# Router gates carried through the one-hot products, a state decay on ScalarE, and a new order at the border

## The chip, the cores and the metric

The kernel runs on one core of a Trainium2 chip. The metric is the device time of one execution in microseconds. Engines are named as in the profile: PE (matrix engine), DVE (VectorE), ACT (ScalarE), POOL (GpSimd) and SP (SyncE, which here only issues DMAs).

## The reference

Linear attention with a decaying state (batch 4, 8 heads, 768 tokens, head dimension 48), then a mixture of experts over its 3072 output rows of 384, with one expert per token and a skip gate:

```python
for t in range(S):
    kt, vt, rt, wt = (k[:, :, t], v[:, :, t], r[:, :, t], w[:, :, t])
    cur = np.einsum('bhd,bhe->bhde', u[None] * kt, vt)
    y[:, :, t] = np.einsum('bhd,bhde->bhe', rt, state + cur)
    state = wt[:, :, :, None] * state + np.einsum('bhd,bhe->bhde', kt, vt)
...
do_compute = x @ w_skip > 0
xc = x[do_compute]
logits = xc @ w_gate
e_idx = np.argmax(logits, axis=1)
probs = softmax(logits)
gate_w = probs[np.arange(len(xc)), e_idx]
for e in range(E):
    mask = e_idx == e
    h = np.maximum(xc[mask] @ w1[e], 0.0)
    y[mask] = gate_w[mask, None] * (h @ w2[e])
out[do_compute] = xc + y
```

Eight experts of 384 x 1024 x 384; w_gate's softmax value of the chosen expert is the token's gate.

## The kernel before

**Attention.** There are 24 steps of 128 tokens (4 sequences of 6 chunks). In each, DVE makes decay products by two scans (L396, L414), POOL and DVE scale r and k with them, PE makes the score quarters (psA, L432), DVE masks them (asb, L448) and adds the bonus (psY, L460), and PE multiplies them with v (L496) and adds the state's part (L502). ACT copies psY to xT (L508). The state lives in PSUM as psu; `update` (L470) adds the chunk's kt v, `carry` (L479) multiplies psu by the next chunk's decay q, and `carry_out` (L488) copies it to SBUF as sblk for the next step's L502. `rows_out` (L517) turns xT into output rows and router logits, which SP stores and later gathers read.

**Router.** Steps are routed in three groups, GROUPS = (0, 12), (12, 6), (18, 6). For each, DVE finds the expert of each token and its rank (sg, rall), one-hot rows of the rank are made (`one_hot`, by DVE, or by ACT as the pair off and hot, L633 and L634), and `places` (L651) multiplies the one-hots, as weights, with sg. The result pt (in PSUM, shown as psu) holds, per expert and rank, the token's index in two parts and a flag that the slot is taken. From it come idr and ids, the index lists of the gathers. The token's gate is 1 / sum of the exponentials; `gate_rows` turns it on PE, copies it on ACT and stores it with SP (L610 to L613) to gd in DRAM, and POOL later gathers it for each of 16 tiles of tokens (`gate`, L548, tiles gt).

**Border.** The last group's router runs after the last step. PE fills it with expert 0's first 128 tokens (L159, then L733), which were found early.

**Experts.** Each has up to 256 tokens in two tiles (xg, gathered by POOL), transposed on PE (L953), split into high and low halves xTh and xTl, and multiplied by the first weights (L977 to L979, or L991 where at most 160 tokens came) and the second (L1001, with L1008 for the few tokens of such an expert: e = 2, 6 and 7). The weights come in by SP (L116), are rounded by ACT (w1h, w2h, L135) and completed by DVE or POOL (w1l, w2l, L139). DVE scales by the gate and adds the row (fin, L1088), POOL scatters it (L962). Order on all engines is the program's order; an engine waits in line.

A tile for a later gather is cleared by DVE when the gather is issued, and loads for expert 2 are tied to an earlier copy:

```python
xg[s] = pool.tile([P, DM], F32, tag=f"xg{s % 2}", name=f"xg{s}", bufs=3)
if s < 10:
    nc.vector.memset(xg[s], 0.0)
...
for load in load_weights(2, q):
    beside(load, copied[1])
```

`flags` (L942, L943) sums two checks by two tiny products into psf; it stands ahead of the last expert's last layer-2 products.

Of the kernel before, what the change touches and what calls it, by code (L numbers as in the profile page):

```python
# [20 lines left out]
P = 128  # L21
# [28 lines left out]
          24: ((1, 2), (1, 3))}  # L50
KEYS_AT = {-2: (), -1: (0,), 0: (1,), 1: (2, 3)}
# [21 lines left out]
NV = 3  # L73
# [6 lines left out]
def rwkv_moe_kernel(ctx, tc, wrk, wrk0, vN, uP, wgs, wgp, w12, cst, out):  # L80
# [3 lines left out]
    gd = dram.tile([NT, 1], F32, name="gd")  # L84
# [65 lines left out]
    gts = [keep.tile([P, 1], F32, name=f"gt{s}") for s in range(2 * E)]  # L150
# [17 lines left out]
    with tc.tile_pool(name="att", bufs=2) as att, \  # L168
# [99 lines left out]
        ids = keep.tile([P, 2, E], U32, name="ids")  # L268
        floor = pss[:, :NP * HW // 2].bitcast(BF16)
# [3 lines left out]
        for nm, wd in (("desc", E), ("mx", MG), ("km", MG), ("sm", MG), ("os1", E), ("rank", MG)):  # L273
            o = 396 + sum(z.shape[1] for z in small.values())
            small[nm] = pss[:, o:o + wd]
        tok_ps = pss[:, 512 - 2 * n:].rearrange("p (c q o) -> p c q o", q=2, o=1)
        gall = pers.tile([P, n], F32, name="gall")
# [197 lines left out]
        def carry(i):  # L475
            b, c = seq[i]
            if c == NC - 1:
                return
            nc.vector.tensor_tensor(psu[:, :, :D], psu[:, :, :D],  # L479
                                    work[i + 1]["q"][:, :, 0:1].to_broadcast([P, NP, D]),  # L480
                                    op=ALU.mult)
# [51 lines left out]

        def gather(s, pool):
            if pool:
                xg[s] = pool.tile([P, DM], F32, tag=f"xg{s % 2}", name=f"xg{s}", bufs=3)
                if s < 10:
                    nc.vector.memset(xg[s], 0.0)  # L538
# [7 lines left out]

        def gate(s, rows, index):
            nc.gpsimd.indirect_dma_start(  # L548
                out=gts[s], out_offset=None, in_=gd[:rows],
                in_offset=bass.IndirectOffsetOnAxis(ap=index, axis=0),  # L550
                bounds_check=rows - 1, oob_is_err=False)

        def router(i0, m):
# [74 lines left out]
            def one_hot(c):  # L628
# [6 lines left out]
                if c in by_act:  # L635
# [11 lines left out]
            def places():  # L647
                placed.append(i0)
                for j in (1, 0):
                    for k, c in enumerate(order):  # L650
                        nc.tensor.matmul(pt[:, j], hots[c][:, j * P:(j + 1) * P],  # L651
                                         sg[:, c], start=False, stop=(k == m - 1),
                                         skip_group_check=True)
            if last:
                held.append(places)
# [6 lines left out]
            sm = by("sm", m, 1)  # L662
            vec.tensor_reduce(sm, ex, axis=AX, op=ALU.add)
            yield 1
            vec.reciprocal(gall[:, i0:i0 + m].rearrange("p (c o) -> p c o", o=1), sm)
            yield 1
            if not last:
                grow()
                rare.extend((places, gate_rows))
            else:  # L670
                held.append(gate_rows)
# [211 lines left out]
        for s in (2, 3):  # L883
            gather(s, None)
# [393 lines left out]
```

## Time and profile before

| | |
|---|---|
| median of 3 runs | 277.79 us (277.7 to 278.22) |
| profiled execution | 277.29 us, its span 275.5 us |
| PE busy | 257.7 us (94%) |
| DVE busy | 226.7 us (82%) |
| POOL busy | 213.6 us (78%) |
| ACT busy | 152.3 us (55%) |

The span is the time from the first to the last instruction that the profiler shows; the 1.79 us around it belong to the execution. Shares are of the span. A PE at 94% leaves about 18 us, of which those at the start and after the last product are outside this change. Times in the rows below are microseconds from the span's start.

### The profile page before, as it was taken

How to read it: one execution, taken by the hardware profiler on the slowest of the kernel's cores; microseconds unless marked ns; L12 is line 12 of the kernel's file. 1: busy time of each engine (PE TensorE's matmuls, PEld its weight loads, DVE VectorE, ACT ScalarE, POOL GpSimd, SP SyncE). 2: the span in 40 equal slices, each digit the busy share in tenths (PEclk: the TensorE clock that was granted, in tenths of full speed). 3: DMA queues.
4: the chain of work that ended last, by engine and by line, in shares of the span. 5: the costliest groups of instructions: out<-in, count | busy, mean ns of one | idle time of the engine just before them, and what ended most of it. 6: DMA issues, size and time to landing. Idle time of an engine off the chain costs nothing.

```text
span 275.5 us, 9346 instructions
## 1 busy us (share of the span) xinstructions
PE 257.7 (94%) x3705; PEld 226.8 (82%) x3706; DVE 226.7 (82%) x428; ACT 152.3 (55%) x376; POOL 213.6 (78%) x199
## 2 busy tenths in 40 slices
PE   7899999999989999998999899999999999999990
PEld 2467878888878878786788899996999999999870
DVE  6998699888899999986284529899999979979960
ACT  6133443433445687453543737385893957959810
POOL 7989989999889798689656822696898989876811
PEclk9999999999999999999999999999999999999997
DMA  6979999999999998587945984439698696984001
GB/s 165 248 204 295 269 279 247 280 254 241 284 255 238 286 266 237 145 271 235 338 158 151 348 334 154 140 80 376 257 335 306 192 353 254 329 293 156 37 6 49
DMA packets 24803, 64.38 MB, mean 234 GB/s; under 512 B 4483, under 2 KB 15779, under 8 KB 23206
## 3 DMA queue, kind: packets, MB, share of 16 engines
q1 hardware_dynamic: 21910, 58.40, 69.6%
q0 software_dynamic: 2560, 4.76, 5.2%
q8 instruction: 39, 0.64, 0.9%
q10 hardware_dynamic: 272, 0.39, 0.5%
q14 instruction: 22, 0.18, 0.2%
HBM read 57.21 MB, written 7.88 MB: 236 GB/s over the span
## 4 chain that ended last, share of the span: by engine, by line
PE 63%; DMA 16%; DVE 10%; issue 6%; ACT 2%; POOL 1%; SPq 1%; POOLq 0%; DVEq 0%; ACTq 0%
PE psO L1001 17%; PE psH L991 7%; PE psY L496 5%; PE psA L432 4%; PE psH L977 4%; PE psH L979 4%; PE psH L978 4%; PE psX L517 4%; DMA wrk<-wrk 4%; PE psY L502 3%; DMA r<-w 3%; DVE asb L448 3%; PE psY L456 3%; DMA xg<-out,ids 2%; PE psT L441 2%
## 5 line engine op out<-in xcount | busy, mean ns | idle before, releaser
L391 POOL TENSOR_TENSOR wrk<-wrk 128x512 f32<-128x512 f32 x24 | 36.2, 1509 | 1.7
L139 DVE TENSOR_TENSOR w1l<-r,w1h 128x512 fp32r<-128x512 f32 x31 | 36.6, 1197 | 0.1
L448 DVE TENSOR_TENSOR asb<-psA,c_sb 128x512 f32<-128x512 f32 x48 | 30.8, 682 | 5.0 <-PE psA L432 4.7
L412 POOL TENSOR_TENSOR kq<-wrk,q 128x512 f32<-128x512 f32 x24 | 26.9, 1120 | 10.0 <-DVE q L396 8.1
L1001 PE MATMUL psO<-w2h,hh 128*128 128x384 f32 x96 | 32.8, 342 | 0.0
L962 POOL DMA_INDIRECT out<-fin,ids x16 | 19.6, 1223 | 17.1 <-DVE fin L1088 6.9
L139 POOL TENSOR_TENSOR w2l<-r,w2h 128x512 fp32r<-128x512 f32 x24 | 31.0, 1313 | 2.3 <-ACT w2h L135 2.0
L508 ACT COPY xT<-psY 128x512 f32<-128x512 f32 x24 | 14.0, 585 | 33.7 <-PE psY L502 25.8
L1001 PE MATMUL psO<-w2l,hh 128*128 128x384 f32 x96 | 32.2, 336 | 0.0
L496 PE MATMUL psY<-asb,vN 128*64 128x128 f32 (+1 forms) x384 | 26.1, 276 | 3.0 <-DVE psY L460 2.9
L384 POOL TENSOR_TENSOR rk<-wrk 128x512 f32<-128x512 f32 x22 | 28.1, 1275 | 0.0
L539 POOL DMA_INDIRECT xg<-out,ids x14 | 17.5, 1253 | 13.3 <-DVE xg L538 9.1
L432 PE MATMUL psA<-rp,kq 64*64 64x128 f32 (+1 forms) x768 | 26.3, 252 | 1.3 <-POOL kq L412 1.3
L135 ACT CAST w2h<-r 128x512 fp32r<-128x512 f32 x48 | 27.3, 655 | 0.0
L977 PE MATMUL psH<-xTh,w1h 128*128 128x224 f32 (+1 forms) x96 | 26.9, 280 | 0.0
L979 PE MATMUL psH<-xTh,w1l 128*128 128x224 f32 (+1 forms) x96 | 26.5, 277 | 0.0
L978 PE MATMUL psH<-xTl,w1h 128*128 128x224 f32 (+1 forms) x96 | 26.5, 276 | 0.0
L135 ACT CAST w1h<-r 128x512 fp32r<-128x512 f32 x42 | 25.6, 632 | 1.6 <-DMA r<-w 1.6
L496 PEld LDWEIGHTS psY<-asb,vN 128*64 128x64 f32 (+1 forms) x384 | 20.4, 130 | 5.3 <-DVE psY L460 4.3
L432 PEld LDWEIGHTS psA<-rp,kq 64*64 64x64 f32 x768 | 21.8, 133 | 3.3 <-POOL kq L412 1.7
L1040 DVE SCALAR_TENSOR_TENSOR hl<-psH,hh 128x512 fp32r<-128x512 f32 (+1 forms) x32 | 20.2, 648 | 4.2 <-ACT hh L1039 3.9
L1039 ACT ACTIVATE hh<-psH 128x512 fp32r<-128x512 f32 (+1 forms) x32 | 18.3, 570 | 9.2 <-PE psH L979 6.5
(179 smaller groups left out, 707.0 us busy)
## 6 DMA issues: line engine op xcount, KB each, us to landing
r<-w SPq DMA_DIRECT2D x12, 1536.0 KB, 7.3
wrk<-wrk SPq DMA_DIRECT2D x23, 577.9 KB, 6.6
r<-w SPq DMA_DIRECT2D x12, 512.0 KB, 7.5
wp<-wrk SPq DMA_DIRECT2D x9, 516.0 KB, 8.6
vN<-vN SPq DMA_DIRECT2D x12, 384.0 KB, 4.7
out<-x SPq DMA_DIRECT2D x24, 192.0 KB, 5.4
vt<-wrk SPq DMA_DIRECT2D x24, 96.0 KB, 6.3
vt<-wrk SPq DMA_DIRECT2D x48, 48.0 KB, 4.6
```

Source lines behind the costliest of these rows:

```text
L135: nc.scalar.copy(hi, raw)
L139: eng.tensor_tensor(lo, raw, hi.bitcast(F32), op=ALU.subtract)
L384: (nc.gpsimd if i > 1 else nc.vector).tensor_tensor(rk.rearrange("p a j -> p (a j)"), t[:, R_OFF:K_OFF], t[:, K_OFF:V_OFF], op=ALU.mult)
L391: nc.gpsimd.tensor_tensor(rk1, rk1, two(1, 1, CW), op=ALU.mult)
L412: nc.gpsimd.tensor_tensor(pairs(kq), pairs(wk["k"]), twice(wk["q"][:, :, 1:HW]), op=ALU.mult)
L432: nc.tensor.matmul(psa[g][j:j + HP, a, j:], wk["kq"][rows, a, j:j + HP], wk["rp"][rows, a, j:], start=True, stop=True)
L448: nc.vector.tensor_tensor(s, psa[g], tri.rearrange("p (o j) -> p o j", o=1).to_broadcast([P, NP, P]), op=ALU.mult)
L496: nc.tensor.matmul(quarter(0, a, g, w), head(i, 2 * a + g, w), wk["asb"][g][:, a], start=False, stop=(c == 0), skip_group_check=True)
L977: nc.tensor.matmul(ps, w1h[:, o:o + P], xh, start=(kc == 0), stop=False)
L978: nc.tensor.matmul(ps, w1h[:, o:o + P], xl, start=False, stop=False)
L979: nc.tensor.matmul(ps, w1l[:, o:o + P], xh, start=False, stop=(kc == KC - 1))
L1001: nc.tensor.matmul(pso, h[j, fc][k], w[:, fc * DM:(fc + 1) * DM], start=(i == 0), stop=(i == len(todo) - 1))
```

## The change

Five edits. (1) In steps 12 to 19 that carry a state (12 to 16, 18, 19) the decay of psu is four ACT activations with a scale per partition in place of one DVE product. (2) The gate is cut into three bf16 values, whose sum is the gate in float precision, and these ride as three more columns times eight experts through the places' products; `gates`, one sum out of PSUM, replaces the rows in DRAM and the 16 gathers. In the last group the first 24 columns go first and the gates' 24 in a second set of products. (3) At the border the first one-hot is made by ACT, ids and the gathers of tiles 2 and 3 follow idr at once. (4) Tiles 6 to 9 are cleared in expert 0, and the loads of expert 2's weights wait for the landing of the third gather. (5) The flags' products stand behind the eighth of the last 24 products.

```diff
+BY_ACT = range(12, 20)
...
-NV = 3
+NV = 6
...
@@ carry
+            q = work[i + 1]["q"]
+            if i in BY_ACT:
+                for a in range(NP):
+                    nc.scalar.activation(psu[:, a, :D], psu[:, a, :D], AF.Copy, scale=q[:, a, 0:1])
+                return
             nc.vector.tensor_tensor(psu[:, :, :D], psu[:, :, :D],
...
+        def token_tile(s, pool):
+            xg[s] = pool.tile([P, DM], F32, tag=f"xg{s % 2}", name=f"xg{s}", bufs=3)
+            if s < 10:
+                nc.vector.memset(xg[s], 0.0)
...
-        def gate(s, rows, index):
-            nc.gpsimd.indirect_dma_start(
-                out=gts[s], out_offset=None, in_=gd[:rows],
...
-            def gate_rows():
-                pg = ps1.tile([P, 512], F32, tag="psT", name=f"pg{i0}", bufs=2)[:m, :P]
-                nc.tensor.transpose(pg, gall[:, i0:i0 + m], ident)
-                row = att.tile([MG, P], F32, tag="gate", name=f"gate{i0}", bufs=1)[:m]
-                nc.scalar.copy(row, pg)
-                nc.sync.dma_start(gd[i0 * P:(i0 + m) * P].rearrange("(c p) o -> c (p o)", p=P), row)
+            def weigh():
+                sm, w = by("sm", m, 1), parts_ps[:, :m]
+                vec.tensor_reduce(sm, ex, axis=AX, op=ALU.add)
+                yield 1
+                vec.reciprocal(w[:, :, 0], sm)
+                yield 1
+                for q in range(2):
+                    part = att.tile([P, MG, 1], BF16, tag=f"part{q}", name=f"part{q}_{i0}")[:, :m]
+                    vec.tensor_copy(part, w[:, :, q])
+                    vec.tensor_tensor(w[:, :, q + 1], w[:, :, q], part, op=ALU.subtract)
+                    yield 1
+                vec.tensor_tensor(
+                    sg[:, :, 3:], oh.rearrange("p c (o e) -> p c o e", o=1)
+                    .to_broadcast([P, m, 3, E]), w.to_broadcast([P, m, 3, E]), op=ALU.mult)
...
-            by_act = () if last else [c for c in range(m) if c % 3 if m == MG or c % 2]
+            by_act = (0,) if last else [c for c in range(m) if c % 3 if m == MG or c % 2]
...
-            def places():
+            def places(a=0, b=NV):
...
             if last:
-                held.append(places)
+                held.append(lambda: places(0, 3))
                 while held:
                     yield 1
...
                 gather(1, None)
+                taken = pt[:, :, 2]
+                vec.tensor_scalar(idf, taken, 0.0, BIG, op0=ALU.is_equal, op1=ALU.mult)
+                vec.tensor_tensor(ids, idf, idr, op=ALU.add)
+                for s in (2, 3):
+                    landed.append(gather(s, None))
+            yield from weigh()
+            if last:
+                held.append(lambda: places(3, NV))
+                while held:
+                    yield 0
+                vec.tensor_reduce(gates, pt[:, :, 3:].rearrange("p j q e -> p j e q"), axis=AX,
+                                  op=ALU.add)
+                return
...
             for i, (k, fc, w) in enumerate(todo):
+                if beside and i == FC:
+                    beside()
...
             if e == 0:
+                for s in range(6, 10):
+                    token_tile(s, moe)
                 scatter(0, fin0)
...
-                nc.vector.scalar_tensor_tensor(o, pso, gts[s], xg[s],
+                nc.vector.scalar_tensor_tensor(o, pso, gates[:, j, e:e + 1], xg[s],
...
-                if s == 2 * E - 1:
-                    flags()
...
-                    beside(load, copied[1])
+                    beside(load, landed[-1])
```

Where instructions stand at the border, on DVE. Before, behind the first index list of the last group (pss is a PSUM scratch, gall the gates, few and size_i the expert sizes):

```order
L285 TENSOR_REDUCE pss<-ex_sb 128x6
L285 RECIPROCAL gall<-pss 128x6
L711 TENSOR_TENSOR h0l<-hf_2693,h0h 128x512
L881 TENSOR_SCALAR idf<-psu 128x16
L882 TENSOR_TENSOR ids<-idf,idr 128x16
L886 TENSOR_SCALAR few<-psu 1x8
L887 SCALAR_TENSOR_TENSOR few<-psu,few 1x8
```

And now, at the same place:

```order
L287 TENSOR_SCALAR idf<-psu 128x16
L287 TENSOR_TENSOR ids<-idf,idr 128x16
L287 TENSOR_REDUCE pss<-ex_sb 128x6
L287 RECIPROCAL pss<-pss 128x6
L287 CAST part_18_2781<-pss 128x6
L287 TENSOR_TENSOR pss<-pss,part_18_2781 128x6
L287 CAST part_18_2785<-pss 128x6
L287 TENSOR_TENSOR pss<-pss,part_18_2785 128x6
L287 TENSOR_TENSOR sg_2710<-sg_2710,pss 128x6x24
L287 TENSOR_REDUCE gates<-psu 128x16
L731 TENSOR_TENSOR h0l<-hf_2701,h0h 128x512
L900 TENSOR_SCALAR few<-psu 1x8
```

The index list of tiles 2 and 3 has moved ahead, and the gates' chain stands ahead of h0l and of the sizes.

On PE, between the last group's places and the first gather's transposes, before (w2h and w2l are expert 0's second weights):

```order
L733 MATMUL psO_2759<-w2h_0_1537,h0h 128x384
L733 MATMUL psO_2759<-w2l_0_1538,h0h 128x384
L733 MATMUL psO_2759<-w2h_0_1537,h0h 128x384
L610 MATMUL pg_2764<-c_sb,gall 6x128
L733 MATMUL psO_2759<-w2l_0_1538,h0h 128x384
L733 MATMUL psO_2759<-w2h_0_1537,h0h 128x384
```

And now:

```order
L753 MATMUL psO_2778<-w2h_0_1524,h0h 128x384
L753 MATMUL psO_2778<-w2l_0_1525,h0h 128x384
L753 MATMUL psO_2778<-w2h_0_1524,h0h 128x384
L753 MATMUL psO_2778<-w2l_0_1525,h0h 128x384
L753 MATMUL psO_2778<-w2h_0_1524,h0h 128x384
L665 LDWEIGHTS hot_0_2728
L665 MATMUL psu<-sg_2710,hot_0_2728 128x24
L665 LDWEIGHTS hot_1_2732
L665 MATMUL psu<-sg_2710,hot_1_2732 128x24
```

The gate transpose after the third product is gone, and after the fifth come twelve products of the one-hots with the gates' columns of sg (four rows of 24 are shown).

On POOL, from the gathers at the border to those of expert 1, before:

```order
L548 DMA gt_72<-gd,id_71 128x1
L539 DMA xg_67<-out,ids 128x384
L539 DMA xg_68<-out,ids 128x384
L539 DMA xg_2847<-out,ids 128x384
L539 DMA xg_2852<-out,ids 128x384
L1110 MEMSET zero 128x384
L139 TENSOR_TENSOR w1l_1_2623<-r_10_2534,w1h_1_2622 128x512
L962 DMA out<-fin_88,ids 3072x384
L548 DMA gt_73<-gd,idr 128x1
L548 DMA gt_74<-gd,idr 128x1
L548 DMA gt_75<-gd,idr 128x1
L962 DMA out<-fin_1_2968,ids 3072x384
```

And now:

```order
L548 DMA xg_66<-out,ids 128x384
L548 DMA xg_67<-out,ids 128x384
L548 DMA xg_2869<-out,ids 128x384
L548 DMA xg_2874<-out,ids 128x384
L1123 MEMSET zero 128x384
L139 TENSOR_TENSOR w1l_1_2632<-r_10_2543,w1h_1_2631 128x512
L976 DMA out<-fin_72,ids 3072x384
L976 DMA out<-fin_1_2989,ids 3072x384
```

The gate gathers (gt) are gone from the queue (16 in the whole program), and what stood behind them has moved up.

## Rows read from the trace of the kernel before

**Rows 1.** The waits of PE: what for, us in total, times, longest.

```profile
PE psY L496 <- DVE psY L460: 2.9, 7, 0.6
```

**Rows 2.** Two stretches: busy time of each engine, then clock granted, DMA share, GB/s.

```profile
96.00:101.10 5.10, 4.52 (x112) 3.72 (x107) 4.98 (x12) 4.37 (x11) 4.75 (x5) 1.00 1.05 275
200.20:264.00 63.80, 63.80 (x462) 60.87 (x461) 57.67 (x76) 48.87 (x110) 51.83 (x41) 1.00 0.69 243
```

**Rows 3.** Groups by line and shape on DVE: busy us, mean ns, idle before.

```profile
L479 DVE TENSOR_TENSOR psu<-psu,q 128x192 f32<-128x192 f32 x20 | 6.8, 342 | 0.0
...
L285 DVE TENSOR_TENSOR sg<-sg,pss 128x192 bf16<-128x192 bf16 x1 | 0.3, 343 | 0.0
```

**Rows 4.** The same view, ACT.

```profile
L488 ACT COPY sblk<-psu 128x192 f32<-128x192 f32 x20 | 6.4, 322 | 3.6 <-DVE psu L479 3.6
L1038 ACT ACTIVATE hf<-psH 128x64 f32<-128x64 f32 x24 | 5.4, 225 | 24.3 <-PE psH L979 13.6 <-PE psH L991 10.7
```

**Rows 5.** The timeline of ACT: start, us, instruction, idle before.

```profile
89.50 0.52 ACT L633 ACTIVATE off<-iota,rall 128x256 bf16<-128x256 bf16 x1
90.05 0.51 ACT L634 ACTIVATE hot<-off,bias_one 128x256 bf16<-128x256 bf16 x1
...
134.05 1.14 ACT L135 CAST w1h<-r 128x512 fp32r<-128x512 f32 x2 [1.64 <-DMA r<-w]
```

**Rows 6.** The waits of SyncE's DMA queue.

```profile
SPq L613 <- ACT gate L612: 11.1, 3, 6.2
```

**Rows 7.** The timeline of PE, end of the attention and border.

```profile
135.72 0.40 PE L517 MATMUL psX<-wgp_sb,xT 128*64 128x105 f32 x4 [0.48 <-ACT xT L508]
...
143.40 0.34 PE L733 MATMUL psO<-w2h,h0h 128*128 128x384 f32 x1
...
146.85 0.52 PE L703 MATMUL psX<-c_sb,xg 128*128 128x128 f32 x3 [0.47 <-DMA xg<-out,idr]
...
154.66 0.55 PE L953 MATMUL psX<-c_sb,xg 128*128 128x128 f32 x3 [0.77 <-DMA xg<-out,ids]
```

**Rows 8.** Group by line and shape, PE: places.

```profile
L651 PE MATMUL psu<-sg,hot 128*128 128x24 bf16 x48 | 2.1, 174 | 0.4
```

**Rows 9.** The timeline of DVE, border.

```profile
137.47 0.20 DVE L285 TENSOR_TENSOR dl<-lg,pss 128x48 f32<-128x48 f32 x1
137.71 0.20 DVE L285 SCALAR_TENSOR_TENSOR key<-dl,pss 128x48 f32<-128x48 f32 x1
...
142.41 0.19 DVE L285 TENSOR_REDUCE idr<-psu 128x16 uint32<-128x32 f32 x1 [0.50 <-PE psu L651]
```

**Rows 10.** The timeline of POOL, border and experts 1 and 2.

```profile
147.79 1.00 POOL L539 DMA_INDIRECT xg<-out,ids  x1 [0.30 <-issue]
...
174.10 1.59 POOL L539 DMA_INDIRECT xg<-out,ids  x1 [6.97 <-DVE xg L538]
...
187.21 1.30 POOL L139 TENSOR_TENSOR w1l<-r,w1h 128x512 fp32r<-128x512 f32 x1
```

**Rows 11.** The timeline of DVE, expert 1.

```profile
170.61 0.67 DVE L139 TENSOR_TENSOR w1l<-r,w1h 128x512 fp32r<-128x512 f32 x1
...
186.81 2.25 DVE L139 TENSOR_TENSOR w1l<-r,w1h 128x512 fp32r<-128x512 f32 x1
```

**Rows 12.** The timeline of PE, ahead of expert 2 and in the tail.

```profile
188.28 0.83 PE L1008 MATMUL psO<-r,hf 128*32 128x384 f32 x2
189.68 0.52 PE L1008 MATMUL psX<-r,hf 128*32 128x384 f32 x3 [0.57 <-DVE xTl L957]
...
191.10 0.37 PE L977 MATMUL psH<-xTh,w1h 128*128 128x224 f32 x1
...
262.74 0.51 PE L1008 MATMUL psO<-r,hf 128*32 128x384 f32 x1
...
264.05 0.19 PE L942 MATMUL psf<-viol,rows 128*1 128x1 f32 x2
264.68 0.19 PE L943 MATMUL psf<-vt,c_sb 128*1 128x1 f32 x2 [0.44 <-DVE vt L937]
```

More of the change, by code (lines that the diff above doesn't have):

```diff
@@ L149, in rwkv_moe_kernel @@
     id0 = keep.tile([P, 1], U32, name="id0")
-    gts = [keep.tile([P, 1], F32, name=f"gt{s}") for s in range(2 * E)]
+    gates = keep.tile([P, 2, E], F32, name="gates")
     fin0 = keep.tile([P, DM], F32, name="fin0")
@@ L268, in rwkv_moe_kernel @@
         ids = keep.tile([P, 2, E], U32, name="ids")
+        idf = keep.tile([P, 2, E], F32, name="idf")
+        landed = []
         floor = pss[:, :NP * HW // 2].bitcast(BF16)
@@ L272, in rwkv_moe_kernel @@
         small = {}
-        for nm, wd in (("desc", E), ("mx", MG), ("km", MG), ("sm", MG), ("os1", E), ("rank", MG)):
-            o = 396 + sum(z.shape[1] for z in small.values())
+        for nm, o, wd in (("desc", 396, E), ("mx", 404, MG), ("rank", 404, MG), ("os1", 404, E),
+                          ("km", 416, MG), ("sm", 416, MG)):
             small[nm] = pss[:, o:o + wd]
+        parts_ps = pss[:, 428:428 + 3 * MG].rearrange("p (q c o) -> p c q o", q=3, o=1)
         tok_ps = pss[:, 512 - 2 * n:].rearrange("p (c q o) -> p c q o", q=2, o=1)
-        gall = pers.tile([P, n], F32, name="gall")
         by = lambda nm, m, w: small[nm][:, :m * w].rearrange("p (c e) -> p c e", e=w)
@@ L532, in store @@
             nc.sync.dma_start(out[i * P:(i + 1) * P], x.rearrange("p a g d -> p (a g d)"))
+        def token_tile(s, pool):
+            xg[s] = pool.tile([P, DM], F32, tag=f"xg{s % 2}", name=f"xg{s}", bufs=3)
+            if s < 10:
+                nc.vector.memset(xg[s], 0.0)
         def gather(s, pool):
[L535 to L538, printed above, removed]
+            if pool and s not in xg:
+                token_tile(s, pool)
             rows = nc.gpsimd.indirect_dma_start(
@@ L545, in gather @@
                 own_rows(rows)
-        def gate(s, rows, index):
-            nc.gpsimd.indirect_dma_start(
-                out=gts[s], out_offset=None, in_=gd[:rows],
-                in_offset=bass.IndirectOffsetOnAxis(ap=index, axis=0),
-                bounds_check=rows - 1, oob_is_err=False)
+            return rows
         def router(i0, m):
@@ L634, in rows @@
                     nc.scalar.activation(hot, off, AF.Relu, bias=bias_one, scale=-1.0)
-                if c in by_act:
+                if c in by_act and last:
+                    rows()
+                elif c in by_act:
                     rare.append(rows)
@@ L661, in router @@
                 gather(1, None)
-            sm = by("sm", m, 1)
-            vec.tensor_reduce(sm, ex, axis=AX, op=ALU.add)
-            yield 1
[L665 to L671, printed above, removed]
+                taken = pt[:, :, 2]
[11 more added lines that the diff above has]
+                return
+            grow()
+            yield 1
+            rare.extend((lambda: None, places) if i0 else (places,))
             yield 1
@@ L735, in early_expert @@
                 yield 160
-            nc.vector.scalar_tensor_tensor(fin0, pso, gts[0], xg[0], op0=ALU.mult, op1=ALU.add)
+            nc.vector.scalar_tensor_tensor(fin0, pso, gates[:, 0, 0:1], xg[0], op0=ALU.mult, op1=ALU.add)
         def pad(k):
@@ L866, in rwkv_moe_kernel @@
             flush()
-        idf = keep.tile([P, 2, E], F32, name="idf")
         few = keep.tile([P, E], F32, name="few")
@@ L878, in rwkv_moe_kernel @@
         early_low(1)
-        gate(0, LATE * P, id0)
         taken = pt[:, :, 2]
-        nc.vector.tensor_scalar(idf, taken, 0.0, BIG, op0=ALU.is_equal, op1=ALU.mult)
-        nc.vector.tensor_tensor(ids, idf, idr, op=ALU.add)
-        for s in (2, 3):
-            gather(s, None)
         step, sizes = few[FEW - P:FEW - P + 1], size_i[FEW - P:FEW - P + 1]
@@ L994, in layer1, with layer2 @@
                 larger()
-        def layer2(e, j, h, pso):
+        def layer2(e, j, h, pso, beside=None):
             w2h, w2l = wsp[e, 2], wsp[e, 3]
@@ L1064, in expert @@
                     gather(s, moe)
-            if e < E - 1:
-                for s in (2 * e + 2, 2 * e + 3) if e else (1, 2, 3):
-                    gate(s, NT, idr[:, s % 2, s // 2:s // 2 + 1])
             for k, j in enumerate((1,) if e == 0 else (1, 0) if e == E - 1 else (0, 1)):
```

12 lines of the change are left out of this document (5 added, 7 removed).

## The prediction

> **What bounds the kernel now.** I read the waits of the matrix engine (PE) first, because the order on every engine is fixed by the program and PE is the engine that almost never rests. In the busy shares of the stretch from 200.20 to 264 it works 63.80 of 63.80 us [rows 2]: there, in experts 3 to 7, nothing that another engine gains can shorten anything. So the change can only win where PE waits, and I went to those places. In the attention steps the seven waits for VectorE's bonus product come to 2.9 us, 0.6 at most [rows 1]; VectorE (DVE) is busy 4.98 of the 5.10 us of such a step, PE 4.52 and ScalarE (ACT) 4.37 [rows 2]. At the border between attention and experts PE waits 0.48 for an xT copy, 0.47 for the first gather and 0.77 for the third [rows 7]. Ahead of expert 2 the few-token matmuls of L1008 stretch from 188.28 to 191.10, 2.82 us, while the same work before the tail go from 262.74 to 264.05, 1.31 us: 1.51 of the former is stall, of which the table shows 0.57 as a wait for DVE's xTl [rows 12]. In the tail the second flag matmul waits 0.44 [rows 12]. All of this is about 6.5 us, the most that can be won.
>
> **The decay by ScalarE (seven steps).** One DVE product of 0.342 us leaves each of steps 12 to 16, 18 and 19 [rows 3]; the next instruction overlaps its tail, so about 0.25 is freed per step. ACT gets four activations of 48 columns instead, each waiting for the one before. No row shows this operation. From below, a 64-column activation out of PSUM takes 0.225; from above, the copy of the same 192 columns whole takes 0.322 [rows 4], as if width saved nothing. The chained pair off and hot shows that a dependent successor starts 0.55 after one of 0.52, so 0.03 is added [rows 5]. Four make 1.0 to 1.4 us; I take 1.0, by the nearest row in width. In a full step this takes ACT from 4.37 to about 5.4 of 5.10, but two of the activations there (off and hot) can slide, and VectorE's share falls. A late sblk is needed only by the next step's L502, and a late kt by the update of the state, which stands behind the matmuls that waited for VectorE anyway: this is the cover, about 1.1 us in a full step (the 5.10 - 4.37 that ACT has free there, and the 0.34 that VectorE no longer spends), and what sticks out of it lengthens each of the seven steps. I price steps 12 to 16 at 5 x 0.25 gained, of which the PE waits there can return 1.0.
> The Trainium skill ("ScalarE: Activation LUTs", Rules for kernel authors) speaks against this edit: multiply on VectorE, and budget some 0.3 us an activation plus 0.83 ns an element, which is an estimate of 0.34 each and 1.36 a step; no run so far shows these, and by it about 0.3 would stick out of the cover in each step, up to 2 us over the sum below, where the sum by the copies' rows has nothing.
>
> **The gates in the places' products.** Per router group DVE gains a cast, a difference, a cast, a difference and the wide product. A chain of small dependent DVE instructions advances 0.24 each (137.47 to 137.71) [rows 9]; the product over 12x24 elements I put at 0.45 and over 6x24 at 0.3, the first from 0.343 for 192 elements [rows 3] by the larger count, the second just below that row. Less the part of the old product that goes, the first group pays about 1.3 us of DVE in step 17 and the second about 1.1 in step 20. Group 0 eats the 1.0 just won; of group 1 about 0.3 stays, since kq comes late once. The 36 matmuls twice as wide cost nearly nothing more: all 48 old ones together take 2.1 us, 0.04 each [rows 8].
> The three gate rows (PE transpose, ACT copy, store) leave. SyncE's queue stood in front of the stores for 11.1 us in three waits, 6.2 the longest [rows 6], and the expert weights stand behind it. Without the stores they come sooner, and the w1h casts that began at 134.05 after 1.64 of waiting for their load [rows 5] no longer hold up the xT for which PE waits until 135.72: minus 0.48 [rows 7]. All attention together: -1.0 +1.0 +0.3 -0.5, **-0.2** at the border.
>
> **The border.** The first one-hot of the last group goes to ACT and takes one of six off DVE: places, and idr at 142.41 [rows 9], are 0.3 sooner, and one L159 matmul goes behind, 0.2 more. idr stands then at 141.9. Behind it come idf, ids, the sum, the reciprocal, four conversions and the product: nine steps of 0.24 and 0.3, ready at 144.2 to 144.3. PE stands in order: it has five L733 products (the fifth began at 143.40 and took 0.17 of its slot [rows 7]; now done at 143.0), then twelve second place matmuls that need the product. So it waits about 1.2 and spends 12 x 2.1/48 = 0.5. Before, PE reached the first gather's transposes at 146.85 - 0.47 = 146.38; now at 146.38 - 0.5 - 0.2 + 1.2 + 0.5 - 0.2 (the slot of the gate transpose, counted like its neighbours' 0.17) = 147.2, later than the landing, so that the 0.47 is inside this. **+0.35.** What is queued behind this wait on PE are eleven products and everything after; behind it on DVE the sum of the gates, both h0l and size_i, which all come about 2 us later, still ahead of the last eight L733.
> Gathers 2 and 3 now go out right behind the first, without the gate gather between and without waiting for anything: some 2 us before 147.79 [rows 10]. The old third took until 154.66 [rows 7], behind weight loads issued just after it; these now wait for its landing. Issued at 145.5 or so (idr at 141.9, a microsecond to start, two gathers of 1.00 + 0.30) and even with the old 6.8 from issue to landing it is there at 152.3, before PE comes to it near 154, so the 0.77 goes: **-0.8**. With this PE enters expert 0's second product **0.65** sooner.
>
> **Expert 2's stall.** The first xTl ends near 189.6 and frees a PSUM tile that L1008 needs [rows 12]. DVE is late because its w1l products beside GpSimd's products of the same form take 2.25 (the one at 186.81, while GpSimd's ran from 187.21) instead of 0.67 [rows 10, 11]; there are three such between 180 and 189. GpSimd ran these late as its gather at 174.10 waited 6.97 for DVE's memset [rows 10] and two gate gathers followed. Both go: memsets move to expert 0, gate gathers vanish. The three excesses (3 x 1.58 = 4.7 us) move into earlier stretches where DVE has slack. DVE must gain the 1.5 of the stall and the 0.65 of PE's own advance, 2.15 of the 4.7; I count the stall as gone: **-1.5**, least certain of the large terms (bounds: 0 and -1.5).
>
> **Flags.** The pair moves behind eight of 24 products. Before, its second began at 264.68, 0.63 after its first, with the 0.44 inside [rows 12]; amid the products the wait goes and the two slots close up. **-0.5.**
>
> **The sum** is -0.2 +0.35 -0.8 -1.5 -0.5 = -2.65 on the profiled execution's 277.29: 274.6. The median of the runs lies 0.5 above that execution: **275.1**.
>
> **The rivals.**
> *Expert 2's stall stays, wholly or in half.* GpSimd's w2l products don't vanish; they fall on VectorE's own w1l and w2l of 172 to 180 and push these back, and the last w1l still meets one: +0.75 to +1.5, **275.9 to 276.6**. For it: such an overlap costs DVE 1.58 [rows 10, 11]; against it: 4.7 us are freed and 2.15 needed.
> The Trainium skill ("SBUF — State Buffer", Who interferes with whom) has the rule behind this: a VectorE instruction with two SBUF inputs contends with a GpSimd one that reads SBUF; the trace agrees (2.25 beside 0.67), and by it the cost moves with the overlap and is not removed, which is this rival's time.
> *ScalarE becomes the bound (the other side).* If the four activations cost so much that sblk and kt come after their cover, PE waits in each of seven steps. Out of the cover of 1.1, each 0.1 an activation is 7 x 4 x 0.1 = 2.8 us in all; the whole gain of 2.65 is gone at 0.37 each. At my upper bound of 0.35 the time is 275.1 + 2.1 = 277.2, at 0.40 it is 278.6: **277.2 to 278.6**. For it: ACT's 4.37 of 5.10 [rows 2]; against: the row nearest in width, 0.225 [rows 4].
> *The border is dearer.* If the product is ready half a microsecond later, or size_i, which PE's sequencer reads just before the gather's transposes, holds it, PE gives back 0.5 to 1.0: **275.6 to 276.1**.
> *The attention gains more*: VectorE's wide products fit in its gaps (its waits for PE), then 1.0 stays: **274.1**.
>
> **How the numbers follow.** Likeliest sum 0.50 (own range 274.3 to 275.9), stall stays 0.20, border dearer 0.12, more gain 0.10, ScalarE the bound 0.08. Of the last, half lands within 0.2% of before (0.56 us, about what runs of this kernel can tell from no change) and half above; the others are all faster but for a few in a hundred where two combine. Faster 0.89, same 0.06, slower 0.05. The range 273.6 to 276.9 leaves out the ScalarE case and half a tenth on the other side.
>
> **What will show it.** Right if: the activations of the decay last about 0.22 and PE shows no wait on sblk or kt in steps 13 to 20; PE waits about 1.2 at the second place matmuls for the product of DVE, and no longer at the third gather; L1008 ahead of expert 2 lasts 1.3 to 1.5; the flag matmuls show no wait. Wrong if a wait of PE on ACT of 0.3 or more recurs each step, if the wait for the product passes 1.7, or if DVE's w1l of 2 us stand ahead of expert 2 again.

## The result and the profile after

The changed kernel takes 275.42 us in the median of 4 runs (273.64 to 276.29), the kernel before 278.0 in 4 runs (277.7 to 279.38). The ratio is 0.9876, 95% interval 0.983 to 0.9921: faster by 1.2%. The profiled execution took 275.95 with a span of 274.2. A second measurement of the same kernel on another occasion (run e12 below) gave 0.9878, 0.9829 to 0.9926. Runs over 1.5% above the fastest of their kernel count in the medians below, but not in the ratios and their intervals.

The first part of the page after, busy us, share and count of each engine. VectorE's busy time fell by 10.8 us and GpSimd's by 18.2, ScalarE's grew by 7.4, PE's stayed:

```profile
PE 257.3 (94%) x3714; PEld 226.9 (83%) x3715; DVE 215.9 (79%) x436; ACT 159.7 (58%) x403; POOL 195.4 (71%) x183
```

PE's waits, where [rows 1] stood at 2.9 us: VectorE's bonus product is still waited for, now nine times; new are, above all, the wide product of the gates at the border and the kt copy. The waits for the third gather, the first gather, xTl, xT at 135.72 and the flags' sum are gone:

```profile
PE psY L502 <- DVE psY L462: 3.6, 9, 0.7
...
PE psu L665 <- DVE sg L287: 0.7, 1, 0.7
...
PE pr L588 <- ACT kt L445: 0.7, 1, 0.7
```

The second stretch of [rows 2] after. PE is as full as it was from 200.20 on (63.80 of 63.80):

```profile
200.20:264.00 63.80, 63.80 (x462) 60.91 (x461) 48.98 (x79) 48.52 (x110) 35.60 (x28) 1.00 0.68 237
```

ScalarE's new operation, to set beside the copy of [rows 4], and VectorE's widest new product, beside [rows 3] (busy us, mean ns, idle before):

```profile
L484 ACT ACTIVATE psu<-psu,q 128x48 f32<-128x48 f32 x28 | 7.8, 277 | 0.7
```

```profile
L287 DVE TENSOR_TENSOR sg<-sg,pss 128x288 bf16<-128x288 bf16 x1 | 0.5, 454 | 0.0
```

The activation of 48 columns takes 0.277 us, the wide product 0.454 for the twelve steps of the first group; the two for six steps take 0.304 in the mean. PE's timeline after, at the places of [rows 7] and [rows 12], ahead of them the router's products of step 18:

```profile
110.71 0.18 PE L588 MATMUL pr<-sg,trib 128*128 128x48 bf16 x1 [0.67 <-ACT kt L445]
...
144.68 0.33 PE L753 MATMUL psO<-w2h,h0h 128*128 128x384 f32 x1
145.75 0.45 PE L665 MATMUL psu<-sg,hot 128*128 128x24 bf16 x12 [0.74 <-DVE sg L287]
...
148.87 0.52 PE L723 MATMUL psX<-c_sb,xg 128*128 128x128 f32 x3
...
155.42 0.82 PE L967 MATMUL psX<-c_sb,xg 128*128 128x128 f32 x6
...
189.32 0.51 PE L1024 MATMUL psO<-r,hf 128*32 128x384 f32 x1
...
190.75 0.37 PE L991 MATMUL psH<-xTh,w1h 128*128 128x224 f32 x1
...
265.09 0.19 PE L956 MATMUL psf<-viol,rows 128*1 128x1 f32 x2
265.14 0.19 PE L957 MATMUL psf<-vt,c_sb 128*1 128x1 f32 x2
```

The second places wait 0.74 for the product, the transposes of the first and the third gather (148.87, 155.42) wait for nothing, L1024 ahead of expert 2 takes 1.43 us (189.32 to 190.75) where L1008 took 2.82, and the flag pair stands 0.05 apart. VectorE's and GpSimd's timelines at the places of [rows 9 to 11]:

```profile
143.71 0.19 DVE L287 TENSOR_REDUCE idr<-psu 128x16 uint32<-128x32 f32 x1 [0.50 <-PE psu L665]
...
145.39 0.30 DVE L287 TENSOR_TENSOR sg<-sg,pss 128x144 bf16<-128x144 bf16 x1
...
160.45 0.62 DVE L1103 SCALAR_TENSOR_TENSOR fin<-psO,gates,xg 128x384 f32<-128x384 f32 x1 [0.20 <-PE psO L1017]
...
181.06 0.68 DVE L139 TENSOR_TENSOR w1l<-r,w1h 128x512 fp32r<-128x512 f32 x1
...
186.61 0.56 DVE L971 TENSOR_TENSOR xTl<-psX,xTh 128x384 fp32r<-128x384 f32 x1
```

```profile
146.80 1.11 POOL L548 DMA_INDIRECT xg<-out,ids  x1 [0.30 <-issue]
...
176.13 2.53 POOL L139 TENSOR_TENSOR w2l<-r,w2h 128x512 fp32r<-128x512 f32 x2
```

The wide product is ready at 145.7, fin no longer waits for a gate, the w1l product takes 0.68, and GpSimd's products run between 172.8 and 178.7 and from 181.6 to 182.9, instead of between 180.4 and 188.5.

The order of work is the same in every kernel, so stretches between the same instructions can be compared. Starts are read from the timelines: xT is ScalarE's copy of a step, "gather 1" PE's transposes L703 (after: L723), "e0" the first of expert 0's products L1001, "few" the first L1008 (after: L1024) ahead of expert 2, "tail" the first such product of the last expert, "last" the last hl products.

| stretch, us | before | after | e1 | e2 | e3 | e7 | e10 | e11 | e12 |
|---|---|---|---|---|---|---|---|---|---|
| start to xT 12 (same code) | 74.97 | 75.93 | 74.97 | 74.79 | 74.74 | 75.39 | 75.04 | 74.79 | 77.65 |
| xT 12 to 17 | 26.14 | 26.16 | 26.16 | 26.42 | 26.18 | 26.16 | 26.16 | 26.17 | 26.16 |
| xT 17 to 20 | 16.64 | 17.21 | 17.61 | 17.47 | 17.37 | 17.22 | 16.89 | 17.20 | 17.20 |
| xT 20 to 22 | 11.40 | 12.04 | 11.41 | 12.06 | 12.04 | 12.05 | 11.39 | 11.89 | 12.05 |
| xT 22 to 23 | 5.94 | 5.29 | 6.36 | 5.30 | 5.29 | 5.29 | 5.57 | 5.29 | 5.30 |
| xT 23 to gather 1 | 11.76 | 12.24 | 11.93 | 12.28 | 12.25 | 11.51 | 11.73 | 11.50 | 12.27 |
| gather 1 to e0 | 8.11 | 7.13 | 7.95 | 7.12 | 7.12 | 7.12 | 7.09 | 7.12 | 7.13 |
| few to expert 2 | 2.82 | 1.43 | 2.85 | 1.42 | 1.43 | 1.43 | 1.43 | 1.42 | 1.43 |
| expert 2 to last | 76.60 | 76.03 | 76.77 | 76.15 | 76.03 | 76.04 | 76.04 | 76.19 | 76.41 |
| of it, tail to last | 4.96 | 4.73 | 4.95 | 4.74 | 4.73 | 4.73 | 4.74 | 4.73 | 4.73 |

Between e0 and few lie 33.32 us before and after. Most stretches of one kernel repeat within some hundredths (not the one from expert 2 on, which e12 has 0.38 longer), while the first row, whose code nobody touched, lies between 74.74 and 77.65. So the runs are judged by stretches, and the total by its interval.

### The profile page after: what moved, and what is told of

Read it like the earlier page. It is cut to its first block, busy times and chain, and to the rows that moved or that the text cites. A ratio compares the mean times of both kernels' runs of the same rounds, so it can differ in the third digit from the quotient of the medians.

```text
span 274.2 us, 9351 instructions
## 1 busy us (share of the span) xinstructions
PE 257.3 (94%) x3714; PEld 226.9 (83%) x3715; DVE 215.9 (79%) x436; ACT 159.7 (58%) x403; POOL 195.4 (71%) x183
## 3 DMA queue, kind: packets, MB, share of 16 engines
HBM read 57.20 MB, written 7.86 MB: 237 GB/s over the span
## 4 chain that ended last, share of the span: by engine, by line
PE 72%; DVE 13%; DMA 8%; issue 3%; ACT 2%; POOL 1%; SPq 0%; POOLq 0%; DVEq 0%; ACTq 0%
PE psO L1017 18%; PE psH L1005 7%; PE psY L502 6%; PE psA L434 5%; PE psX L523 4%; PE psH L991 4%; PE psH L993 4%; PE psH L992 4%; PE psH L159 3%; PE psY L508 3%; DVE asb L450 3%; DMA out<-x 3%; PE psY L458 3%; PE psT L443 3%; DMA vt<-wrk 2%
## 5 line engine op out<-in xcount | busy, mean ns | idle before, releaser
L139 POOL TENSOR_TENSOR w2l<-r,w2h 128x512 fp32r<-128x512 f32 x24 | 33.1, 1401 | 22.5 <-ACT w2h L135 22.3
L139 DVE TENSOR_TENSOR w1l<-r,w1h 128x512 fp32r<-128x512 f32 x31 | 24.6, 810 | 0.1
L548 POOL DMA_INDIRECT xg<-out,ids x14 | 15.6, 1114 | 7.3 <-PE psH L159 4.1
```

The lines of the kernel that those rows point to most:

```text
L139: eng.tensor_tensor(lo, raw, hi.bitcast(F32), op=ALU.subtract)
```

## The experiments

**e1, the decay alone.** The kernel before with

```diff
+BY_ACT = range(12, 20)
...
+            if i in BY_ACT:
+                for a in range(NP):
+                    nc.scalar.activation(psu[:, a, :D], psu[:, a, :D], AF.Copy, scale=q[:, a, 0:1])
+                return
```

> The kernel before with one edit: the decay of psu by four ScalarE activations in steps 12 to 16, 18 and 19. The prediction's theory: VectorE gives back 0.25 a step, PE's waits for it shrink, 1.0 us less at the xT of step 17 and about 0.7 less in all. Rival A, from the profile after: the decay only stood where the read product waits for the scan anyway, so VectorE gains 0.1 a step or less, and in step 18 PE waits some 0.5 us for the late kt of ScalarE; in sum within 0.3 us of before. Rival B, ScalarE as the bound: 2 us more, waits of PE on ScalarE in each of the seven steps.

Measured: 279.23 (12 runs) against 279.31 for before (23 runs), ratio 1.0011 (0.9973 to 1.0049). The xT of step 17 comes as late as before (26.16 to 26.14): 0.25 is won up to step 16 (20.79 for 21.04) and lost in the next (5.37 for 5.10). From 17 to 20 it is 0.97 longer. PE's timeline there (PEld is PE's loading of weights):

```profile
100.58 0.20 PEld L507 LDWEIGHTS psY<-rp,sblk 64*64 64x64 f32 x8 [0.34 <-issue]
```

```profile
104.91 0.67 PE L471 MATMUL psu<-vN,kt 128*64 128x48 f32 x16 [1.02 <-DVE dl L286]
...
110.12 0.18 PE L589 MATMUL pr<-sg,trib 128*128 128x48 bf16 x1 [0.75 <-ACT kt L444]
```

The 0.75 at 110.12 is the kt of step 18, late on ScalarE, as rival A had it. The other two are not the decay's. The 0.34 at 100.58 is a pause for nothing that the profile shows, in step 17, where the lead of PE was lost: its product with v had begun 0.33 sooner than before (99.03 for 99.36). The 1.02 at 104.91 stands ahead of the update of psu, which needs kt, a load of v and VectorE's clearing of psu; kt was there at 103.64 and the clearing ended at 99.55, so by exclusion it was the load, whose landing the trace doesn't show. No other profile of this study has this wait; 0.66 of the 0.97 lies in this step. The 0.42 more from step 22 to 23 is a wait of 0.90 for xT, behind weight loads, where the kernel before has 0.48. At the xT of step 20 this run stands 0.99 behind the kernel before; without the 0.34 and the 0.66 about nothing is left. This agrees with rival A, as an estimate from one profile: alone, the decay on ScalarE is worth about nothing to the kernel before, and it isn't the bound that rival B said.

**e2, the decay undone** in the changed kernel: `BY_ACT = ()`.

> The changed kernel with the decay back on VectorE in all steps, the rest as changed. The prediction's theory: 1.0 us slower than the changed kernel at step 17. Rival A: step 17 within 0.3 us, the 0.67 us wait of PE for kt in step 18 gone and at most 0.2 left, so the same or up to 0.4 us faster in all. Rival B: 2 us faster.

Measured: 275.5 (6 runs), ratio to before 0.9852 (0.9807 to 0.9896); the total can't tell it from the changed kernel. By stretches it is 0.26 longer to step 17 and another 0.26 longer to step 20. PE's waits there:

```profile
99.46 1.09 PE L502 MATMUL psY<-asb,vN 128*64 128x128 f32 x16 [0.84 <-DVE psY L462]
...
109.53 0.18 PE L588 MATMUL pr<-sg,trib 128*128 128x48 bf16 x1 [0.25 <-ACT kt L445]
```

The wait for kt falls to 0.25, as expected, but the waits for VectorE's psY grow: 0.64, 0.84 and 0.78 in steps 16 to 18 and 0.82 in step 20 (0.35, 0.75, 0.68 and 0.25 in the changed kernel). Rival A said the same or faster; it is slower by 0.52, and the prediction's 1.0 is twice too much. Together with e1: once VectorE carries the gates' chain, the decay on ScalarE returns half a microsecond; without the chain it returns about nothing.

**e3, the decay in five steps:** `BY_ACT = range(12, 17)`.

> The changed kernel with ScalarE's decay in steps 12 to 16 alone. If steps 18 and 19 are the ones that cost (rival A), PE's wait for kt of 0.67 us in step 18 is gone and the time from the xT of step 17 to that of step 20 is about 0.4 us shorter than in the changed kernel, with the time up to step 17 as there. If the decay pays in every step, this is 0.5 us slower than the changed kernel.

Measured: 274.88 (6 runs), ratio 0.9827 (0.978 to 0.9875). The wait in step 18 is 0.25 instead of 0.67, but from 17 to 20 it takes 17.37, 0.16 more than the changed kernel: in step 20 PE waits 0.82 for VectorE instead of 0.25. What the late kt costs in step 18 VectorE's head start gives back by step 20. Neither expected sign holds in full: steps 18 and 19 pay, but 0.16 and not 0.5.

**e4, the flags alone:** the kernel before with `flags` called from `layer2` behind the eighth product.

> The kernel before with one edit: the two flag products behind the eighth of the last 24 products. Theory: the 0.44 us wait of the second flag product goes and the last products end 0.5 us sooner, 277.3. Rival: VectorE's end (fin, and the flag itself) sets the end, so that nothing changes: 277.8.

Measured: 278.6 (12 runs), ratio 0.9987 (0.9946 to 1.0028), unclear by the total; its profile has 1.5 us of other waits of PE near 199 (0.91 without a cause that the profile shows, 0.57 for a gather). PE's timeline from the tail to the last products, in the kernel before (it starts at 262.74 [rows 12]) and in e4:

```profile
267.70 1.55 PE L1001 MATMUL psO<-w2h,hl 128*128 128x384 f32 x8
```

```profile
262.70 0.51 PE L1010 MATMUL psO<-r,hf 128*32 128x384 f32 x1
...
267.43 1.55 PE L1003 MATMUL psO<-w2h,hl 128*128 128x384 f32 x8
```

The pair stands 0.05 apart and the wait of 0.44 is gone, as in the changed kernel. From the tail to the last products it takes 4.73 instead of 4.96, so the edit is worth 0.23: the wait goes, but amid the products the pair still takes a place. The figure repeats: 4.95 and 4.96 with the pair at its old place, 4.73 or 4.74 in all twelve profiles with the new one. VectorE's last fin keeps pace (6.32 after the tail, for 6.55), so e4's rival doesn't hold. The changed kernel's whole stretch from expert 2 on is 0.57 shorter (76.03 for 76.60); the other 0.34 lies ahead of the tail and is not the flags'.

**e5, e6 and e9: what held VectorE ahead of expert 2.** In e5 the clearing goes back to the gathers (the loop over `token_tile` in expert 0 is left out); in e6 gate gathers stand again in GpSimd's queue, and in e9 both.

```diff
+            if e < E - 1:
+                for s in (2 * e + 2, 2 * e + 3) if e else (1, 2, 3):
+                    gate(s, NT, idr[:, s % 2, s // 2:s // 2 + 1])
```

> The changed kernel with the clearing of tiles 6 to 9 back at their gathers (experts 1 and 2). Theory of the prediction, that the memsets' wait held GpSimd's queue and pushed its products onto VectorE's: the two gathers wait for VectorE until about 172 and GpSimd's second-weight products start 2 to 3 us later; with VectorE free of the gate wait at its first fin, about half of the stall ahead of expert 2 comes back, 0.4 to 1.0 us. Rival: with the gate gathers gone VectorE reaches the memsets early enough, and nothing comes back (0.0 to 0.2).

> The changed kernel with fifteen gate gathers put back into GpSimd's queue at their old places; they read the first weights with the same indices, and nothing waits for what they bring. Theory: GpSimd's products come 2.5 to 3 us later and meet VectorE's w1l products again, but fin no longer waits 5 us for a gate; 0.3 to 0.8 us of the stall ahead of expert 2 comes back. Rival 1: only the wait of fin for its gate made VectorE late, and nothing comes back. Rival 2: the queue alone made the stall, and all of it, 1.4 us, comes back.

> The changed kernel with both put back: the clearing of tiles 6 to 9 at their gathers, and fifteen gate gathers in GpSimd's queue whose values nothing waits for. Each alone left L1024 ahead of expert 2 at 1.42 us. Theory: only together do they push GpSimd's second-weight products from 176 to 180 and later, where they meet VectorE's three w1l products; most of the stall comes back, from the first L1024 to the first product of expert 2 some 2.3 to 2.8 us. Rival: what made VectorE late was fin's wait for its gate, 7 us, which is still gone; the stretch stays at 1.4 to 1.6.

Measured: 276.12 (8 runs, ratio 0.9914, 0.9886 to 0.9942), 276.43 (7 runs, 0.9931, 0.9901 to 0.996) and 276.13 (6 runs, 0.9889, 0.9843 to 0.9935). From few to expert 2 it takes 1.43, 1.42 and 1.43: no stall in any. In e6 the gathers fit into GpSimd's idle time and its products run as in the changed kernel. In e5 and e9 these products do come late. VectorE in e9, and GpSimd:

```profile
177.67 2.10 DVE L139 TENSOR_TENSOR w2l<-r,w2h 128x512 fp32r<-128x512 f32 x1
...
180.30 3.47 DVE L139 TENSOR_TENSOR w1l<-r,w1h 128x512 fp32r<-128x512 f32 x1
...
184.89 1.65 DVE L139 TENSOR_TENSOR w1l<-r,w1h 128x512 fp32r<-128x512 f32 x1
...
187.66 1.01 DVE L979 TENSOR_TENSOR xTl<-psX,xTh 128x384 fp32r<-128x384 f32 x2
```

```profile
177.93 1.29 POOL L139 TENSOR_TENSOR w2l<-r,w2h 128x512 fp32r<-128x512 f32 x1
...
180.71 2.50 POOL L139 TENSOR_TENSOR w2l<-r,w2h 128x512 fp32r<-128x512 f32 x2
```

VectorE's three products take 2.10, 3.47 and 1.65 instead of 0.68, 5.2 us too much in all, about as much as in the kernel before (2.27, 2.90 and 2.25, 5.4 too much). Yet xTl starts at 187.66 and its first half ends about 0.2 us before PE comes to it: its few-token products (L1032 in e9) begin at 188.38. So the collision that the prediction named is real, and by itself not enough. The kernel before had one thing more, fin's wait in expert 1. The first row is of the kernel before; the second is of e4, whose code is the same there, and names what was waited for, the gathered gate (e1 names it too):

```profile
163.69 0.62 DVE L1088 SCALAR_TENSOR_TENSOR fin<-psO,gt,xg 128x384 f32<-128x384 f32 x1 [6.99 <-PE psH L979]
```

```profile
162.52 0.62 DVE L1090 SCALAR_TENSOR_TENSOR fin<-psO,gt,xg 128x384 f32<-128x384 f32 x1 [6.88 <-DMA gt<-gd,idr]
```

VectorE had made up for this wait before the collision began: in the kernel before it waits for ScalarE again at 179.39, as in the changed kernel at 180.45, both 8.9 ahead of few and both for 1.16. What the wait still moved is GpSimd's queue. VectorE's clearing of the tile stands 14.83 ahead of few in the kernel before and 16.99 in e9, and GpSimd's products follow. VectorE, then GpSimd, in the kernel before, and GpSimd in e4:

```profile
179.39 0.69 DVE L1040 SCALAR_TENSOR_TENSOR hl<-psH,hh 128x512 fp32r<-128x512 f32 x1 [1.16 <-ACT hh L1039]
```

```profile
180.42 1.29 POOL L139 TENSOR_TENSOR w2l<-r,w2h 128x512 fp32r<-128x512 f32 x1
```

```profile
178.83 1.29 POOL L139 TENSOR_TENSOR w2l<-r,w2h 128x512 fp32r<-128x512 f32 x1
```

| | before | e1 | e4 | e9 | e5 | e6, after |
|---|---|---|---|---|---|---|
| GpSimd's first w2l ahead of few, us | 7.86 | 7.84 | 8.40 | 10.45 | 13.02 | 16.49 |
| few to expert 2, us | 2.82 | 2.85 | 2.28 | 1.43 | 1.43 | 1.42, 1.43 |

The kernel before, e1 and e4 have the same code here. In e4 the queue is 0.54 earlier, most of it because one gate gather took 1.00 instead of 1.43, and the stall is 0.54 shorter. So the later GpSimd's products meet VectorE's, the less room is left before xTl: the collision makes the stall, and the late queue decides it. Putting fin's wait back by itself was not tried. From expert 2 to the last products e9 takes 77.00 instead of 76.03, with 0.48 of it a wait for a gather; the 0.2 to 0.3 of e5 and e6 is less than the 0.38 by which e12, the changed kernel itself, is longer.

**e7, the second places later.** The gates' products and their sum are kept until 20 of the 24 products at the border are issued.

```diff
-                held.append(lambda: places(3, NV))
-                while held:
-                    yield 0
-                vec.tensor_reduce(gates, ...
+                def gates_in():
+                    places(3, NV)
+                    vec.tensor_reduce(gates, ...
+                ends.append(gates_in)
...
         for k in range(done[0], 6 * FC - 4):
             next(todo)
+        ends.pop()()
```

> The changed kernel with the gates' second set of place products and their sum moved behind the first 20 of PE's products of expert 0 at the border (from behind the fifth). Theory: PE's wait of 0.74 us for the wide product goes, and with it 0.7 us of the time at the first gather's transposes. Rival: the wait only moves, to the size that PE's sequencer reads, to h0l or to the gather's landing, and less than 0.3 us is gained.

Measured: 275.05 (6 runs), ratio 0.9901 (0.9863 to 0.994). From xT 23 to the first gather's transposes it takes 11.51 instead of 12.24. PE's timeline between has no other wait than these:

```profile
142.18 0.91 PE L665 MATMUL psu<-sg,hot 128*128 128x24 bf16 x12 [0.16 <-ACT hot L646]
...
147.62 0.52 PE L723 MATMUL psX<-c_sb,xg 128*128 128x128 f32 x3 [0.20 <-PE psu L665]
```

The 0.74 became a gain of 0.73, as the theory had it; of the versions that keep the gate in three values, this and e11 are the shortest from the xT of step 12 to the last products (190.14 and 190.12, for 190.85 of the changed kernel), though the total alone can't show 0.7.

**e8, the loads untied:** `beside(load, copied[1])` for `landed[-1]`.

> The changed kernel with expert 2's weight loads tied to the earlier copy again instead of to the third gather's landing. Theory of the prediction: the gathers go out 2 us earlier, and even at the old 6.8 us from issue to landing they come before PE: no wait, the same time within 0.2 us. Rival: the landing is so late beside the loads that PE waits again, 0.3 to 0.8 us more.

Measured: 275.3 (6 runs), ratio 0.9891 (0.986 to 0.9923); gather 1 to e0 takes 7.12, as in the changed kernel. The earlier issue does it all; the tie is worth nothing here.

**e10, one bf16 value.** `NV = 4`, no casts and differences, the product 8 wide: the gates are rounded to bf16.

> The changed kernel with the gate as one bf16 value (four columns of eight in place of six): the casts and differences are left out and the product is 8 instead of 24 wide, so the gates are rounded to bf16. Theory: VectorE's chain is what costs in the attention, 0.57 from the xT of step 17 to 20 and 0.57 from 20 to 21; here both stretches come back to 16.7 (with the decay's wait in step 18 perhaps 17.0) and 5.3, and at the border the wide product's wait is 0.3 instead of 0.74. Rival: the decay on ScalarE costs these, then the stretch 17 to 20 stays at 17.2.

Measured: 274.1 (6 runs), ratio 0.9809 (0.9761 to 0.9857). From 17 to 20 it takes 16.89, 0.32 less than the changed kernel, and from 20 to 22 11.39, 0.65 less, as in the kernel before. PE waits for kt and for the narrower product:

```profile
109.52 0.18 PE L588 MATMUL pr<-sg,trib 128*128 128x48 bf16 x1 [0.84 <-ACT kt L445]
...
143.27 0.44 PE L660 MATMUL psu<-sg,hot 128*128 128x8 bf16 x12 [0.35 <-DVE sg L287]
```

So the casts, the differences and the wider product cost 0.97 up to step 22 in the changed kernel, and 0.35 of the 0.74 remains at the border without them. From 22 to 23 e10 loses 0.28 again, in which PE waits 0.23 for the early gather, so 0.69 is left at step 23. The wait for kt stays, and with it 0.25 over the kernel before.

**e11, e7 with the decay of steps 20 to 22 on ScalarE too:** `BY_ACT = range(12, 23)`.

> The changed kernel with the late second places of the run e7 and ScalarE's decay in steps 20 to 22 as well, where ScalarE waits 1 to 2 us a step. Theory: VectorE gains up to 0.25 in step 21, where PE waits 0.25 for its mask, so 0.2 to 0.3 less at the xT of step 22 than e7, and the border as in e7: 0.9 to 1.0 below the changed kernel. Rival: ScalarE's late sblk or kt takes its place and the stretch from the xT of step 20 to that of 23 is the same or longer (17.3).

Measured: 275.22 (6 runs), ratio 0.9853 (0.9805 to 0.99). From 20 to 22 it takes 11.89, 0.16 less than e7; expert 2 to last takes 0.15 more, within what e12 shows of that stretch. The theory's sign holds, its size is halved.

**e12, the changed kernel again.**

> The changed kernel once more, beside the others on one chip: the stretches between the xT of step 12 and the last products agree with those of the first profile within 0.1 us each, while the time up to step 12, where the code is that of before, differs by up to 1 us.

Measured: 276.36 (6 runs, 274.8 to 278.17). All stretches from step 12 to expert 2 agree within 0.03; the last is 0.38 longer, so one of the expected agreements failed. The first row is 1.72 longer. PE's timeline there:

```profile
51.59 0.38 PE L472 MATMUL psu<-vN,kt 128*64 128x48 f32 x6 [1.62 <-issue]
```

## Why the prediction was right

**The total.** 275.1 was forecast and 275.42 measured. From the xT of step 12 to the last products the two profiles differ by 192.73 - 190.85 = 1.88, where the sum had 2.65; the end of the span was 0.38 sooner after, and the untouched start 0.96 later. Single runs of either kernel lie 1.7 to 2.7 us apart, and the repeat e12 has a median of 276.36; so that the median came out within 0.4 of the forecast is in part luck. The terms are what can be judged. By the stretches they are: attention +0.58 (for -0.2), border +0.48 (+0.35), gathers -0.98 (-0.8), the stall -1.39 (-1.5), flags -0.23 (-0.5), and -0.34 between expert 2 and the tail, which no term had and which e12 doesn't show.

**The decay (-1.0): mis-sized.** The step that failed is "about 0.25 is freed per step". Where VectorE's carry stood before, in step 16:

```profile
95.88 0.70 DVE L414 TENSOR_TENSOR_SCAN pss<-p,pss 128x260 f32<-128x260 f32 x1
96.49 0.34 DVE L479 TENSOR_TENSOR psu<-psu,q 128x192 f32<-128x192 f32 x1
96.74 0.22 DVE L285 RECIPROCAL gall<-pss 128x12 f32<-128x12 f32 x1
96.88 0.63 DVE L419 TENSOR_TENSOR rp<-wrk,pss 128x512 f32<-128x512 f32 x1
```

In e1, where nothing but the carry is gone:

```profile
95.66 0.70 DVE L415 TENSOR_TENSOR_SCAN pss<-p,pss 128x260 f32<-128x260 f32 x1
96.40 0.23 DVE L286 RECIPROCAL gall<-pss 128x12 f32<-128x12 f32 x1
96.55 0.63 DVE L420 TENSOR_TENSOR rp<-wrk,pss 128x512 f32<-128x512 f32 x1
```

And in the changed kernel:

```profile
96.61 0.70 DVE L416 TENSOR_TENSOR_SCAN pss<-p,pss 128x260 f32<-128x260 f32 x1
97.35 0.24 DVE L287 RECIPROCAL pss<-pss 128x12 f32<-128x12 f32 x1
97.69 0.69 DVE L421 TENSOR_TENSOR rp<-wrk,pss 128x512 f32<-128x512 f32 x1
```

From the start of the scan to the read product it takes 1.00 before and 0.89 in e1: 0.11 is freed, not 0.25. The other four steps say the same (1.02 to 0.91 twice, 1.23 to 1.12, 1.19 to 1.08). The carry began 0.61 after the scan's start, while what comes next without it begins 0.74 after: most of the carry had stood in a gap. In the changed kernel it is 1.08, and 1.18 in e2: again 0.1, but there the reciprocal writes pss and the read product begins 0.34 behind it, not 0.15. Five times 0.11 is 0.55. PE's product with v of step 17 begins 0.33 sooner in e1 than before, and 0.37 sooner in the changed kernel than in e2, each counted from the xT of step 12. So about a third of the 1.0 was won there. ScalarE's price was 1.21 us for four (107.59 below), 0.30 each, between the bounds and above the 1.0 chosen. ScalarE in step 18:

```profile
107.59 1.21 ACT L484 ACTIVATE psu<-psu,q 128x48 f32<-128x48 f32 x4
...
110.10 0.56 ACT L445 COPY kt<-psT 128x512 f32<-128x512 f32 x1
```

kt begins at 110.10, behind the decay, sblk, off and hot; PE wants it 0.67 before 110.71. The cover held in six of the seven steps and failed here.

**The gates' chain (+1.0 and +0.3).** Measured +0.57 from 17 to 20 and +0.64 from 20 to 22. The second is twice its term: in step 20 the chain stands ahead of VectorE's scan, and PE waits 0.50 for GpSimd's kq behind it. e10 takes 0.97 of these 1.21 away. The decay's gain is inside these figures: e2, which has the chain and not the decay, stands 1.11 behind the kernel before at step 20 and loses 0.66 more up to step 22. So the first term was near, the second half of what it cost, and the decay returned 0.5 instead of 1.0: the attention up to step 22 lost 1.23 instead of 0.3.

**The weights' loads (-0.48):** -0.65 from 22 to 23, and PE's wait for that xT is gone.

**The border (+0.35):** +0.48. PE's wait was 0.74 and not 1.2, since the five products began no sooner: ScalarE's one-hot made the first places wait 0.16 and more of L159 came ahead of them. The product was ready 1.98 after idr, for the 2.35 worked out.

**The gathers (-0.8):** -0.98.

**Expert 2's stall (-1.5):** -1.39, and the reason was right but for one link. The prediction put the stall on the collision of GpSimd's and VectorE's products, and that on the memset and the gate gathers; e9 brings all of these back and no stall. What it left out is why the memset was late: VectorE had waited 7 us for a gathered gate. In e9, without that wait, the memset comes 2.16 us sooner and GpSimd's products 2.59, and about the same excess is made up for. The rival's picture, the collision moved ahead, is what e5 and e9 show, and no stall came of it.

**The flags (-0.5): mis-sized too.** It was -0.23. The wait of 0.44 went, but of "the two slots close up" only a part came: the pair moved in among the products and still costs there.

**The rivals.** ScalarE as the bound of seven steps did not come; in one step it was, for 0.67. The border was 0.13 dearer. Of the two places in the Trainium skill, "ScalarE: Activation LUTs" (Rules for kernel authors) is not borne out here: an activation of 48 columns took 0.277 of engine and 0.30 with its successor, against the estimate of 0.34; the cover was passed in one step, not in each; and in the changed kernel the product is 0.5 cheaper on ScalarE than on VectorE (e2). The contention of "SBUF — State Buffer" (Who interferes with whom) in the Trainium skill is: products of VectorE and GpSimd that met took VectorE up to 3.47 instead of 0.68 (e9). What the prediction drew from it, that the cost only moves, is not what the changed kernel shows: between 172 and 188 no w1l or w2l product of VectorE takes more than 0.68, though one of GpSimd's takes 1.82.

## What to carry to other kernels

An operation that is taken off a busy engine frees only what its neighbours can't fill (here 0.11 of 0.34): look at whether it stood in the gap between an instruction and the one that needs its result, and count starts, not durations. A chain of small dependent instructions costs its whole length where the next engine's work stands behind it; put what waits for it (here the second places) where its result is old. And whether two streams of work that collide cost anything depends on when they meet: put the supposed causes back one by one and then together, and compare, in all runs, how far one engine is ahead of the other. The chance differences between runs of the same code are an experiment too.

## What the runs showed of the hardware

In code that no kernel here changed, PE waits near 50 and 57 us for nothing that the profile shows: 1.62 and 1.08 in e12, 0.60 and 0.53 in the first profile of the same kernel, one of 0.26 in e7, one of 0.33 in e4, and none there in the profile of the kernel before, which has one of 0.60 at 28.08 (0.19 in the changed kernel). This alone is most of the 1.72 between two profiles of one kernel, and more than most edits here are worth. Its cause stays open.

An activation of 48 columns from PSUM to PSUM takes 0.277, longer than one of 64 columns from PSUM to SBUF (0.225, [rows 4]).
